# Eight v chains and all imaginary-row chains in pairs on 64 rows each, and the gate product on GpSimd and ScalarE

## The chip, the cores and the metric

The kernel runs on one core of one Trainium2 chip. The core has TensorE for matmuls (PE in the profile, with its weight loads as PEld), VectorE (DVE), ScalarE (ACT), GpSimd (POOL) and SyncE (SP), which issues most DMAs. The metric is the device time of the core in microseconds (us), the median of several executions; less is better.

## The reference, and what is computed

Two branches over the same x (2048 tokens, 512 wide) are mixed by a gate. Cut to what matters:

```
g = sigmoid((x * gate_w).sum(-1, keepdims=True))
a = x @ dft_hid_re.T ;  b = x @ dft_hid_im.T            # per token
y = dft_seq_re @ a - dft_seq_im @ b                     # over the 2048 tokens
q, k, v = split(x @ wqkv)                               # 32 heads of 16
o = softmax(q k^T / 4) v ;  m = o @ wo
out = g * y + (1 - g) * m
```

The places that the change touches are `v`, the rows `b` ("imaginary rows") and the sum inside the gate. The softmax here needs row maxima of the scores, which the kernel computes by separate score matmuls and reductions ("maxima").

## The kernel before, in words

The order of all instructions is written out by hand (`tc.manual_schedule()`): each engine works through its instructions in the order in which the Python code emits them, and the framework adds the waits between engines. All of an engine's later work stands behind an instruction that waits.

Products of float32 precision are made from three matmuls of a reduced type: each operand is split into a high part and a low part (`hi_lo`, L73 to L76: ScalarE casts the high part, VectorE or GpSimd subtracts it for the low part), and `mm3` (L78 to L81) multiplies high with high, high with low and low with high. A *chain* is the 12 matmuls of one tile of 128 tokens by 512 columns: 4 slices of the inner dimension times 3, summed in one PSUM bank.

The stages, in order: the q and k rows (until about 95 us); then, in lines 235 to 304, the part that is changed; then a long main part (from L573 on) in which the Fourier matmuls run on one half of TensorE's 128 rows while score matmuls run on the other half (`Chain.mm`, L339 to L345, slices 64 rows), with a wait put in by hand at the first matmul of each segment; then an end.

The part that is changed runs two loops over the 16 token tiles, s = 0 to 15:

- L259 to L268, the v chains. Each uses all 128 rows and a bank of `psS` (3 banks). ScalarE (L267) and VectorE (L268) each copy one half of the bank into `vt`.
- L280 to L301, the chains of imaginary rows. The same matmuls with other weights (`wch`, `wcl`). Then, in the order of emission: `hi_lo` of the bank into a tile `bt` (ScalarE casts, VectorE subtracts), a store of `bt` to DRAM (512 KB, SP), a load of a gate row block `xa[s + 2]` (256 KB, SP), and the gate product of block s by one VectorE instruction that multiplies and sums (L293). For s = 2 to 5 one slice of `wo` is split as well into a tile `wt` (ScalarE casts, GpSimd subtracts), stored, and only then is the next slice of `wo` loaded (L294 to L299). For s = 6 to 9 `split(1)` does one slice of the real Fourier weights, `wre` (cast on ScalarE, subtract on GpSimd); the first of these calls also issues the loads of all four. `bt` and `wt` share a pool name, `hl`, with two buffers.

From the eleventh v chain on, `visit` (L247 to L257) follows each chain ahead of its evacuation: it emits the score matmuls of two maxima tiles for both heads (four matmuls of 48 rows, those of head 0 on rows 0 to 47 and those of head 1 on rows 64 to 111) and their four reductions on VectorE (`a_tile`, L197 to L211). There are 22 visits, 44 maxima tiles (`LEAD`). Three of the four score banks are of `psA`, the fourth is the bank of `psD`. After 32 tiles the maxima of a half are complete, and two deferred steps (`m_parts`, `m_rows`) spread them into the stacks `qs`.

After the last chain, L302 runs what is deferred, and the main part begins with six matmuls at L343 on all 128 rows into the bank `psD`.

Of the kernel before, what the change touches and what calls it, by code (L numbers as in the profile page):

```python
# [9 lines left out]
F32 = mybir.dt.float32  # L10
F32R = mybir.dt.float32r
AF = mybir.ActivationFunctionType
ALU = mybir.AluOpType
AX = mybir.AxisListType

P = 128
S = 2048
D = 512
# [3 lines left out]
KT = D // P  # L22
NT = S // P
UNITS = NP * 32
LEAD = 44
# [6 lines left out]
def mix_kernel(ctx: ExitStack, tc: tile.TileContext, xa_t, xa, wqkv, w_hid, w_seq, wo, gate_w, out):  # L32
# [5 lines left out]
    nc = tc.nc  # L38
    ctx.enter_context(tc.manual_schedule())

    psS = ctx.enter_context(tc.tile_pool(name="psS", bufs=3, space=PSUM))
    psA = ctx.enter_context(tc.tile_pool(name="psA", bufs=3, space=PSUM))
    psO = ctx.enter_context(tc.tile_pool(name="psO", bufs=1, space=PSUM))
    psD = ctx.enter_context(tc.tile_pool(name="psD", bufs=1, space=PSUM))
# [6 lines left out]
    b_d = [dram.tile([P, 2, D], F32, name=f"b{s}") for s in range(NT)]  # L51
# [4 lines left out]
    wo_d = [dram.tile([P, 2, D], F32, name=f"wo{kt}") for kt in range(KT)]  # L56
# [5 lines left out]
    z = const.tile([P, NT], F32, name="z")  # L62
# [8 lines left out]
    xab = [const.tile([P, 4, 2, D], F32R, name=f"xab{tb}", tag=f"xab{tb}") for tb in range(4)]  # L71
    acc = psO.tile([P, 512], F32, name="acc")

    def hi_lo(hi, lo, src, lo_eng=None):
        nc.scalar.copy(hi, src)  # L75
        (lo_eng or nc.vector).tensor_tensor(lo, src, hi.bitcast(F32), ALU.subtract)  # L76

    def mm3(ps, sh, sl, mh, ml, first, last):  # L78
        nc.tensor.matmul(ps, sh, mh, start=first, stop=False)  # L79
        nc.tensor.matmul(ps, sh, ml, start=False, stop=False)  # L80
        nc.tensor.matmul(ps, sl, mh, start=False, stop=last)  # L81

    right = tc.tile_pool(name="st1", bufs=1, side="right", reuse_waits="tile")
    st1 = right.__enter__()
    wv = [[const.tile([P, D], F32R, name=f"wv{v}{kt}", tag=f"w{4 * v + kt}") for kt in range(KT)] for v in range(2)]
    wch = st1.tile([P, KT, D], F32R, name="wch")
    wcl = st1.tile([P, KT, D], F32R, name="wcl")

    gwb = st1.tile([P, D], F32, name="gwb")
# [3 lines left out]
    def staged(src):  # L93
        raw = st1.tile([P, D], F32, name="raw", bufs=RAW)
        nc.sync.dma_start(raw, src)
        return raw
# [4 lines left out]
    def load_ahead():  # L101
        while todo and len(loaded) < RAW - 1:
            hi, lo, src, lo_eng, shape = todo.pop(0)
            loaded.append((hi, lo, staged(src), lo_eng, shape))

    def split(n):

        for _ in range(n):
            load_ahead()
            if loaded:  # L110
                hi, lo, raw, lo_eng, shape = loaded.pop(0)
                hi_lo(hi, lo, raw.rearrange("p (s t) -> p s t", s=4) if shape else raw, lo_eng)
            load_ahead()
# [7 lines left out]
    def bank():  # L121
        nonlocal banks
        banks += 1
        return (psS if banks % 2 else psA).tile([P, 512], F32, name="s" if banks % 2 else "a")


    with tc.tile_pool(name="qk", bufs=1, reuse_waits="tile") as pool:
        wh = pool.tile([P, 2, KT, D], F32R, name="wh")
        wl = pool.tile([P, 2, KT, D], F32R, name="wl")
# [27 lines left out]
        for tb in range(4):  # L157
            for c in range(2):
# [9 lines left out]
                for ct in range(4):  # L168
                    ps = bank()
# [25 lines left out]
    deferred = []  # L195
    a_left = {}

    def a_tile(i, h, ps=None):
        p, j = divmod(i, 64)
        qt, kb = divmod(j, 4)  # L200
        if ps is None:
            ps = psA.tile([P, 512], F32, name="a")
        r = slice(64 * h, 64 * h + 48)
        nc.tensor.matmul(ps, qs[p % 2][r, qt * P:(qt + 1) * P], ks[p % 2][r, kb * 512:(kb + 1) * 512],  # L204
                         start=True, stop=True)
        user = nc.vector.tensor_reduce(mx[p % 2][:, h, qt, kb:kb + 1], ps, AX.X, ALU.max)  # L206
        hf = j // 32
        a_left[p, hf] = a_left.get((p, hf), 64) - 1
        if not a_left[p, hf]:
            deferred.extend((partial(m_parts, p, hf), partial(m_rows, p, hf)))  # L210
        return user  # L211
# [18 lines left out]
    def run_deferred():  # L230
        while deferred:
            deferred.pop(0)()


    ones = st1.tile([2, 2 * D], F32, name="hl", bufs=2)
    nc.gpsimd.memset(ones, 1.0)
    nc.gpsimd.memset(vt[:, :, :, 16:17], 1.0)
    for i in range(2):
# [3 lines left out]
    xgs = {s: staged(xa[s]) for s in range(2)}  # L242
    wos = [staged(wo[:, 0])]
    load_stacks(0)
    a_next = 0

    def visit(i):  # L247

        nonlocal a_next
        if i < 10 or a_next == LEAD:  # L250
            return
        if deferred:
            deferred.pop(0)()
        for j in range(2):
            for h in range(2):
                a_tile(a_next, h, psD.tile([P, 512], F32, name="d") if j and h else None)
            a_next += 1  # L257

    for s in range(NT):  # L259
        t = xab[s // 4][:, s % 4]  # L260
        ps = psS.tile([P, 512], F32, name="s")
        for kt in range(KT):
            r = slice(kt * P, (kt + 1) * P)
            mm3(ps, t[:, 0, r], t[:, 1, r], wv[0][kt], wv[1][kt], kt == 0, kt == KT - 1)
        visit(s)
        pv = ps.rearrange("p (r h d) -> p r h d", h=2, d=DH)
        nc.scalar.copy(vt[:, s, :, 0:16], pv[:, :, 0])  # L267
        nc.vector.tensor_copy(vt[:, s, :, 17:33], pv[:, :, 1])  # L268

    def spare(i, dt, name):  # L270

        return const.tile([P, 4, P], dt, name=name, tag=f"w{i}")
# [4 lines left out]
        add(wre[0][kt], wre[1][kt], w_hid[0, :, kt], nc.gpsimd)  # L277

    ab = [xab[s // 4][:, s % 4] for s in range(NT)]
    for s in range(NT):  # L280
        t = ab[s]
        ps = psS.tile([P, 512], F32, name="s")
        for kt in range(KT):
            r = slice(kt * P, (kt + 1) * P)
            mm3(ps, t[:, 0, r], t[:, 1, r], wch[:, kt], wcl[:, kt], kt == 0, kt == KT - 1)
        visit(NT + s)
        bt = st1.tile([P, 2, D], F32R, name="hl", bufs=2)
        hi_lo(bt[:, 0], bt[:, 1], ps)
        nc.sync.dma_start(b_d[s], bt.bitcast(F32))
        if s + 2 < NT:  # L290
            xgs[s + 2] = staged(xa[s + 2])
        xg = xgs.pop(s)
        nc.vector.scalar_tensor_tensor(xg, xg, 1.0, gwb, op0=ALU.mult, op1=ALU.mult, accum_out=z[:, s:s + 1])  # L293
        if 2 <= s < 2 + KT:  # L294
            wt = st1.tile([P, 2, D], F32R, name="hl", bufs=2)
            hi_lo(wt[:, 0], wt[:, 1], wos.pop(0), nc.gpsimd)
            nc.sync.dma_start(wo_d[s - 2], wt.bitcast(F32))
            if s + 1 < 2 + KT:
                wos.append(staged(wo[:, s - 1]))  # L299
        elif s >= 2 + KT:  # L300
            split(1)  # L301
    run_deferred()  # L302
    assert a_next == LEAD
    right.__exit__(None, None, None)
# [108 lines left out]
    oh, yp, wos = {}, {}, []  # L413
# [438 lines left out]
```

## Time and profile before

| | before |
|---|---|
| median of 3 runs | 1758.53 us (1757.90 to 1759.54) |
| the profiled execution, its time | 1756.66 us |
| the profiled execution, its span | 1754.8 us |
| mean granted clock of TensorE | 0.994 |
| PE busy | 1728.3 us (98%) |
| DVE busy | 1366.6 us (78%) |
| ACT busy | 1154.1 us (66%) |
| POOL busy | 447.2 us (25%) |

The profile is of one execution. Busy time counts an instruction from its start to its end; matmuls overlap, so a busy PE is not one at its peak. A timeline row reads: start, duration, engine, line, operation, output <- input, shape, count, and in brackets the idle time of the engine ahead of it and what ended that. A window row gives the busy time of PE, PEld, DVE, ACT and POOL with counts, then the granted clock, the share of the DMA engines and their GB/s. An SPq row is the issue of a DMA, not its landing.

### The profile page before, as it was taken

Reading aid. Unit: us, or ns where it says so; the run is one execution under the profiler, and the core shown is the slowest. Engines: PE = TensorE matmul, PEld = TensorE weight load, DVE = VectorE, ACT = ScalarE, POOL = GpSimd, SP = SyncE. Lnnn points to the kernel's source line nnn. Section 1 sums busy time; section 2 is a strip of 40 time slices with the busy share of each in tenths; the row PEclk is TensorE's granted clock in tenths of the full one; section 3 lists DMA queues with packets and bytes.
Section 4 is the critical chain, followed back from the end, with each engine's and each line's share of the span. In section 5 each row is a group of like instructions: output and inputs, shape, how many; then the busy total and the mean of one; then the engine's idle time right before and its main releaser. Section 6 shows DMA issues by size and latency. Waiting matters only on the chain.

```text
span 1754.8 us, 32881 instructions
## 1 busy us (share of the span) xinstructions
PE 1728.3 (98%) x12721; PEld 1041.1 (59%) x12721; DVE 1366.6 (78%) x2299; ACT 1154.1 (66%) x2258; POOL 447.2 (25%) x561
## 2 busy tenths in 40 slices
PE   8999899999999999999999999999999999999997
PEld 7886554446666666566666665666666656544443
DVE  5228878888888888888888888888888888899933
ACT  5211267776767777777677677776776777677785
POOL 0110222232223233322222243332333343200111
PEclk9999899999999999999999999999999999999998
DMA  9754620314132153414146434224142534560113
GB/s 290 236 111 144 225 35 7 56 26 73 44 69 66 47 114 92 74 54 79 44 74 235 94 116 106 69 62 76 49 80 68 123 97 92 184 148 8 42 41 109
DMA packets 82348, 164.79 MB, mean 94 GB/s; under 512 B 19712, under 2 KB 19968, under 8 KB 78352
## 3 DMA queue, kind: packets, MB, share of 16 engines
q1 hardware_dynamic: 77840, 162.30, 36.5%
q8 instruction: 100, 1.64, 0.4%
q0 software_dynamic: 4352, 0.39, 0.3%
q14 instruction: 56, 0.46, 0.1%
HBM read 107.47 MB, written 54.52 MB: 92 GB/s over the span
## 4 chain that ended last, share of the span: by engine, by line
PE 94%; DVE 2%; ACT 2%; DMA 1%; issue 0%; SPq 0%; POOL 0%; DVEq 0%; ACTq 0%; POOLq 0%
PE d L343 35%; PE acc L635 26%; PE s L626 12%; PE a L204 11%; PE s L79 2%; PE s L80 2%; PE s L81 2%; ACT pt L627 1%; DVE mx L206 1%; PE a L79 1%; PE a L80 1%; PE a L81 1%; DMA b<-hl 1%; PE a L343 1%; ACT y L359 0%
## 5 line engine op out<-in xcount | busy, mean ns | idle before, releaser
L206 DVE TENSOR_REDUCE mx<-a 128x1 f32<-128x512 f32 x2026 | 1244.2, 681 | 243.6 <-PE a L204 229.9
L627 ACT ACTIVATE pt<-s 128x512 f32<-128x512 f32 x2008 | 1026.2, 620 | 392.2 <-PE s L626 323.3
L204 PE MATMUL a<-ks,qs 48*128 48x512 f32 x2026 | 814.1, 419 | 3.7 <-DVE mx L206 3.3
L626 PE MATMUL s<-qs,ks 50*128 50x512 f32 x2008 | 769.9, 413 | 0.8 <-DMA qs<-mt 0.5
L343 PE MATMUL d<-xab,ch 64*128 64x512 f32 x2016 | 648.4, 396 | 0.0
L635 PE MATMUL acc<-pt,vt 128*17 128x512 f32 x4096 | 501.7, 597 | 0.0
L343 PEld LDWEIGHTS d<-xab,ch 64*128 64x128 f32 x2016 | 365.9, 184 | 126.6 <-DVE mx L206 60.4
L626 PEld LDWEIGHTS s<-qs,ks 50*128 50x128 f32 x2008 | 366.6, 184 | 109.6 <-ACT pt L627 29.9
L204 PEld LDWEIGHTS a<-ks,qs 48*128 48x128 f32 x2026 | 366.9, 185 | 78.6 <-DVE mx L206 48.7
L343 PE MATMUL d<-xab,cl 64*128 64x512 f32 x1008 | 399.3, 396 | 0.0
L343 PEld LDWEIGHTS d<-xab,cl 64*128 64x128 f32 x1008 | 185.5, 184 | 65.3 <-DVE mx L206 40.8
L327 POOL CAST ch<-craw 128x512 fp32r<-128x512 f32 x126 | 77.4, 614 | 555.1 <-PE d L343 179.8
L635 PEld LDWEIGHTS acc<-pt,vt 128*17 128x17 f32 x4096 | 90.3, 96 | 205.8 <-issue 205.8
L328 POOL TENSOR_TENSOR cl<-craw,ch 128x512 fp32r<-128x512 f32 x126 | 162.4, 1289 | 10.2
L227 POOL DMA_DIRECT2D qs<-mt x128 | 72.0, 568 | 160.8 <-DVE mt L223 152.3
L343 PE MATMUL d<-wre,xab 64*128 64x512 f32 (+1 forms) x348 | 94.9, 405 | 5.0 <-ACT pt L627 2.5
L343 PEld LDWEIGHTS d<-wre,xab 64*128 64x128 f32 (+1 forms) x348 | 59.9, 185 | 42.5 <-issue 26.1
L343 PE MATMUL d<-wo_hl,o_hl 64*128 64x512 f32 (+1 forms) x261 | 70.9, 397 | 0.0
L343 PEld LDWEIGHTS d<-wo_hl,o_hl 64*128 64x128 f32 (+1 forms) x261 | 47.1, 185 | 15.9 <-issue 12.0
L75 ACT CAST hl<-s 128x512 fp32r<-128x512 f32 x32 | 18.8, 586 | 56.2 <-PE s L81 48.7
L76 DVE TENSOR_TENSOR hl<-s,hl 128x512 fp32r<-128x512 f32 x32 | 22.0, 686 | 32.1 <-ACT hl L75 32.1
L218 POOL CAST nhl<-nm 128x16 fp32r<-128x16 f32 x32 | 6.3, 197 | 150.9 <-DVE nm L215 150.9
(124 smaller groups left out, 930.1 us busy)
## 6 DMA issues: line engine op xcount, KB each, us to landing
craw<-w_seq SPq DMA_DIRECT2D x128, 256.0 KB
qk<-hl SPq DMA_DIRECT2D x32, 512.0 KB
qs<-qk SPq DMA_DIRECT2D x96, 128.0 KB
ks<-qk SPq DMA_DIRECT2D x96, 128.0 KB
b<-hl SPq DMA_DIRECT2D x16, 512.0 KB
xab<-b SPq DMA_DIRECT2D x16, 512.0 KB
o<-oe SPq DMA_DIRECT2D x62, 128.0 KB
oh<-nh SPq DMA_DIRECT2D x12, 512.0 KB
```

Of the source, the lines that this page charges most:

```text
L79: nc.tensor.matmul(ps, sh, mh, start=first, stop=False)
L80: nc.tensor.matmul(ps, sh, ml, start=False, stop=False)
L81: nc.tensor.matmul(ps, sl, mh, start=False, stop=last)
L204: nc.tensor.matmul(ps, qs[p % 2][r, qt * P:(qt + 1) * P], ks[p % 2][r, kb * 512:(kb + 1) * 512], start=True, stop=True)
L206: user = nc.vector.tensor_reduce(mx[p % 2][:, h, qt, kb:kb + 1], ps, AX.X, ALU.max)
L227: (nc.sync, nc.gpsimd)[h].dma_start(rows.rearrange("v (q b c) -> v b q c", q=8, b=4)[:, b], mt[hf][32 * b + h:32 * b + 32:2])
L327: nc.gpsimd.tensor_copy(h1, raw)
L328: nc.gpsimd.tensor_tensor(l1, raw, h1.bitcast(F32), ALU.subtract)
L343: i = nc.tensor.matmul(self.ps, st[r], mv[r], start=not self.begun, stop=stop)
L626: nc.tensor.matmul(ps, ks[p % 2][rr, kt * P:(kt + 1) * P], qs[p % 2][rr, q0:q0 + 512], start=True, stop=True)
L627: return nc.scalar.activation(pts[u][:, 2 * qb + h], ps, AF.Exp, bias=0.0, scale=DH ** -0.5)
L635: nc.tensor.matmul(acc[32 * j:32 * j + 17], vt[:, kt, p, 16 * h:16 * h + 17], pt[:, j], start=kt == 0, stop=kt == NT - 1)
```

## The change

Three things are changed between lines 235 and 302.

1. The v chains of s = 8 to 15 and all 16 imaginary-row chains run in groups of four, A, B, C, D, each with a bank of its own (three of `psS`, and `psD` for s % 4 = 3). Each matmul of 128 rows becomes two of 64 rows. A group has four *phases*: A with B, first half; C with D, first half; A with B, second half; C with D, second half. In a phase 12 steps each issue one matmul of the one chain on one half of the rows and one of the other chain on the other half; in the second half the two chains have changed sides. The first matmul of a second-half phase is given a wait by hand: for the last maxima reduction of the phase before it (two matmuls on different rows but in one bank would otherwise be open at a time).
2. `visit` is gone. Each phase from the second on, 22 of them, has two maxima tiles of both heads inside: after its fourth step and after its tenth. The fourth score bank of a phase is now `acc`.
3. The evacuation of two chains follows the second-half phase, one after the other (`b_done(s)`, then `b_done(s + 1)`). In it the gate product is made by GpSimd (the product) and ScalarE (a copy with a sum) in place of the VectorE instruction. The pool name `hl` has four buffers in place of two.

```diff
-    ones = st1.tile([2, 2 * D], F32, name="hl", bufs=2)
+    ones = st1.tile([2, 2 * D], F32, name="hl", bufs=4)
...
-    def visit(i):
...
+    def x_mm(s, wh, wl):
         t = xab[s // 4][:, s % 4]
-        ps = psS.tile([P, 512], F32, name="s")
         for kt in range(KT):
-            r = slice(kt * P, (kt + 1) * P)
-            mm3(ps, t[:, 0, r], t[:, 1, r], wv[0][kt], wv[1][kt], kt == 0, kt == KT - 1)
-        visit(s)
+            h1, l1 = (t[:, v, kt * P:(kt + 1) * P] for v in range(2))
+            yield from ((h1, wh[kt]), (h1, wl[kt]), (l1, wh[kt]))
...
+    def b_done(s, ps):
+        bt = st1.tile([P, 2, D], F32R, name="hl", bufs=4)
         hi_lo(bt[:, 0], bt[:, 1], ps)
         nc.sync.dma_start(b_d[s], bt.bitcast(F32))
         if s + 2 < NT:
             xgs[s + 2] = staged(xa[s + 2])
         xg = xgs.pop(s)
-        nc.vector.scalar_tensor_tensor(xg, xg, 1.0, gwb, op0=ALU.mult, op1=ALU.mult, accum_out=z[:, s:s + 1])
+        nc.gpsimd.tensor_tensor(xg, xg, gwb, ALU.mult)
+        nc.scalar.activation(xg, xg, AF.Copy, accum_out=z[:, s:s + 1])
         if 2 <= s < 2 + KT:
-            wt = st1.tile([P, 2, D], F32R, name="hl", bufs=2)
+            wt = st1.tile([P, 2, D], F32R, name="hl", bufs=4)
             hi_lo(wt[:, 0], wt[:, 1], wos.pop(0), nc.gpsimd)
             nc.sync.dma_start(wo_d[s - 2], wt.bitcast(F32))
             if s + 1 < 2 + KT:
                 wos.append(staged(wo[:, s - 1]))
         elif s >= 2 + KT:
             split(1)
+
+    made, user = 0, None
+
+    def phase(pair, half, maxima):
+        nonlocal a_next, user
+        before, user = user, None
+        for j in range(12):
+            for x, (ps, ops, done) in enumerate(pair):
+                st, mv = ops[j]
+                r = slice(64 * (half ^ x), 64 * (half ^ x) + 64)
+                i = nc.tensor.matmul(ps, st[r], mv[r], start=not half and not j, stop=half == 1 and j == 11)
+                if not j and not x and half:
+                    tc.add_manual_dep(i.ins, before.ins.name,
+                                      mybir.DependencyInfo(mybir.DependencyClass.Sync, mybir.DependencyReason.DATA))
+            if maxima and j in (3, 9):
+                for h in range(2):
+                    user = a_tile(a_next, h, acc if h and j == 9 else None)
+                a_next += 1
+        if half:
+            for ps, ops, done in pair:
+                done(ps)
+        if deferred:
+            deferred.pop(0)()
+
+    def pairs_of(tiles, wh, wl, done):
+        nonlocal made
+        tiles = list(tiles)
+        for i in range(0, len(tiles), 4):
+            new = []
+            for s in tiles[i:i + 4]:
+                ps = psS.tile([P, 512], F32, name="s") if s % 4 < 3 else psD.tile([P, 512], F32, name="d")
+                new.append((ps, list(x_mm(s, wh, wl)), partial(done, s)))
+            for half in range(2):
+                for pair in (new[:2], new[2:]):
+                    phase(pair, half, 0 < made and a_next < LEAD)
+                    made += 1
+
+    for s in range(8):
...
+    pairs_of(range(8, NT), *wv, v_done)
...
+    pairs_of(range(NT), *([w[:, kt] for kt in range(KT)] for w in (wch, wcl)), b_done)
     run_deferred()
```

More of the change, by code (lines that the diff above doesn't have):

```diff
@@ L245, in mix_kernel, with v_done @@
     a_next = 0
-    def visit(i):
[L249 to L259, printed above, removed]
+    def x_mm(s, wh, wl):
         t = xab[s // 4][:, s % 4]
-        ps = psS.tile([P, 512], F32, name="s")
         for kt in range(KT):
-            r = slice(kt * P, (kt + 1) * P)
-            mm3(ps, t[:, 0, r], t[:, 1, r], wv[0][kt], wv[1][kt], kt == 0, kt == KT - 1)
-        visit(s)
+            h1, l1 = (t[:, v, kt * P:(kt + 1) * P] for v in range(2))
+            yield from ((h1, wh[kt]), (h1, wl[kt]), (l1, wh[kt]))
+    def v_done(s, ps):
         pv = ps.rearrange("p (r h d) -> p r h d", h=2, d=DH)
@@ L268, in mix_kernel @@
         nc.vector.tensor_copy(vt[:, s, :, 17:33], pv[:, :, 1])
+    def b_done(s, ps):
+        bt = st1.tile([P, 2, D], F32R, name="hl", bufs=4)
+        hi_lo(bt[:, 0], bt[:, 1], ps)
+        nc.sync.dma_start(b_d[s], bt.bitcast(F32))
+        if s + 2 < NT:
+            xgs[s + 2] = staged(xa[s + 2])
+        xg = xgs.pop(s)
+        nc.gpsimd.tensor_tensor(xg, xg, gwb, ALU.mult)
+        nc.scalar.activation(xg, xg, AF.Copy, accum_out=z[:, s:s + 1])
+        if 2 <= s < 2 + KT:
+            wt = st1.tile([P, 2, D], F32R, name="hl", bufs=4)
+            hi_lo(wt[:, 0], wt[:, 1], wos.pop(0), nc.gpsimd)
+            nc.sync.dma_start(wo_d[s - 2], wt.bitcast(F32))
+            if s + 1 < 2 + KT:
+                wos.append(staged(wo[:, s - 1]))
+        elif s >= 2 + KT:
+            split(1)
@@ L270, in spare @@
+    for s in range(8):
+        ps = psS.tile([P, 512], F32, name="s")
+        ops = list(x_mm(s, *wv))
+        for i, (st, mv) in enumerate(ops):
+            nc.tensor.matmul(ps, st, mv, start=not i, stop=i == len(ops) - 1)
+        v_done(s, ps)
+    pairs_of(range(8, NT), *wv, v_done)
     def spare(i, dt, name):
@@ L279, in mix_kernel @@
     ab = [xab[s // 4][:, s % 4] for s in range(NT)]
[L280 to L294, printed above, removed]
-            wt = st1.tile([P, 2, D], F32R, name="hl", bufs=2)
[L296 to L301, printed above, removed]
+    pairs_of(range(NT), *([w[:, kt] for kt in range(KT)] for w in (wch, wcl)), b_done)
     run_deferred()
```

## The prediction

> **What bounds the kernel now.** First the chain that ended last, on the page, then the windows over the changed stretch (the columns are the stretch, its length, busy time of PE, PEld, DVE, ACT, POOL, then clock, DMA share and GB/s).
>
> ```profile
> PE 94%; DVE 2%; ACT 2%; DMA 1%; issue 0%; SPq 0%; POOL 0%; DVEq 0%; ACTq 0%; POOLq 0%
> ```
> ```profile
> 124.80:143.60 18.80, 18.80 (x85) 12.66 (x84) 14.18 (x26) 2.30 (x6) 0.00 (x0) 1.00 0.00 1
> 143.60:164.90 21.30, 21.30 (x96) 14.55 (x94) 19.84 (x37) 3.59 (x6) 2.59 (x2) 1.00 0.52 178
> 164.90:194.80 29.90, 26.57 (x81) 16.67 (x80) 19.80 (x39) 6.83 (x12) 8.47 (x9) 0.83 0.73 251
> 194.80:213.85 19.05, 19.05 (x85) 12.66 (x84) 18.48 (x37) 3.53 (x6) 2.33 (x4) 1.00 0.58 194
> 213.85:216.30 2.45, 0.02 (x2) 0.05 (x1) 2.45 (x5) 0.00 (x0) 0.00 (x0) 1.00 0.55 217
> ```
>
> TensorE sets the end (94% of the chain), so what the changed stretch gains or loses reaches the end whole: behind it PE is full. Inside the stretch there are three regimes. In the v chains (first row) PE is full and VectorE has room. In most of the imaginary rows (second and fourth) VectorE is nearly full too. In the middle (third row) PE idles 3.3 us and the clock falls to 0.83. Last, PE waits 2.4 us at the border to the main part.
>
> ```profile
> 121.85 0.39 PE L81 MATMUL s<-wv,xab 128*128 128x512 f32 x1
> ...
> 124.57 0.39 PE L81 MATMUL s<-wv,xab 128*128 128x512 f32 x1
> 124.89 0.73 PE L204 MATMUL a<-ks,qs 48*128 48x512 f32 x3
> ...
> 128.50 0.73 PE L204 MATMUL a<-ks,qs 48*128 48x512 f32 x3
> ```
> ```profile
> 150.26 0.73 PE L204 MATMUL a<-ks,qs 48*128 48x512 f32 x3
> ...
> 153.92 0.73 PE L204 MATMUL a<-ks,qs 48*128 48x512 f32 x3
> ```
>
> A v chain without a visit takes 2.72 us (last matmul to last matmul, 12 at 0.2265); with one 3.61, an imaginary row 3.66. Five chains from 164.90 to 194.80 took 29.9 where 18.3 was due: 11.6 us lost.
>
> **The new phase on PE.** The rate of matmuls side by side on 64 rows is shown by the main part:
>
> ```profile
> 401.68 0.39 PE L343 MATMUL d<-xab,chl 64*128 64x512 f32 x1
> 401.69 0.40 PE L626 MATMUL s<-qs,ks 50*128 50x512 f32 x1
> ...
> 404.47 0.38 PE L343 MATMUL d<-xab,ch 64*128 64x512 f32 x1
> 404.62 0.43 PE L204 MATMUL a<-ks,qs 48*128 48x512 f32 x1
> ```
>
> Both sides go through 12 intervals between the first and the last pair of rows: 2.79 and 2.93 us, so 0.238 per slot of two. That is one full-row matmul plus 5%; the pairing gives the arithmetic itself nothing. What it removes is the change between full and half rows: a visit costs 3.61 - 2.72 = 0.89, of which two slots of maxima are 0.48, so 0.41 goes to the change, 22 times, 9 us. A phase with maxima is 14 slots, 3.33 us, one without 12, 2.86. Eight phases of v (the first without maxima) and 16 of rows (the last without) are 332 slots: 79.0 us. Bounds: 0.2265 gives 75.2, 0.244 gives 81.0; I take the middle, which averages both sides. Only one change of rows is left, about 0.1.
>
> **The wait put in by hand.** The first matmul of a second half waits for the last maxima reduction of the phase before.
>
> ```profile
> 125.42 1.89 DVE L206 TENSOR_REDUCE mx<-a 128x1 f32<-128x512 f32 x3 [2.30 <-PE a L204]
> 127.22 0.68 DVE L206 TENSOR_REDUCE mx<-d 128x1 f32<-128x512 f32 x1
> ```
>
> With VectorE idle (2.30) a reduction begins 0.53 after its score matmul (124.89 to 125.42); they follow each other at 0.60 and the last takes 0.68. So the last of two ends 1.81 after the scores begin. In the new phase the scores after the tenth step are followed by two steps only: 3 slots, 0.71 us. PE then stands 1.1 us, and with the restart (weights not yet loaded; between 0 and 0.2, I take 0.15) 1.25. Behind this instruction, PE being in order, stands everything that PE has. Two waits per group, 6 groups: 12 waits, 15 us if VectorE is never late, less where another stall covers one. Bounds 1.0 and 1.4 each.
>
> So v gives 110 slots, 26.2, plus 4 waits, 5.0: from 116.6 (124.8, the end of the eleventh chain, less three chains) to 148.0, where before the rows began at 143.6. Nothing pays for this 4.4 us: the six visits removed were worth 2.5.
>
> **The gate product.** VectorE is relieved:
>
> ```profile
> 149.54 0.68 DVE L76 TENSOR_TENSOR hl<-s,hl 128x512 fp32r<-128x512 f32 x1
> 150.14 0.68 DVE L293 SCALAR_TENSOR_TENSOR raw<-raw,gwb 128x512 f32<-128x512 f32 x1
> 150.75 0.08 DVE L293 DVE_READ_ACCUMULATOR raw<-raw,gwb 128x1 f32 x1
> 150.79 1.89 DVE L206 TENSOR_REDUCE mx<-a 128x1 f32<-128x512 f32 x3
> ```
>
> It gives up 0.65 a row (150.14 to 150.79), 10.4 us in all. Four reductions, a subtraction and this were 3.65 of the 3.66 period; without it 3.0 a row is left against 3.33 of PE a phase. The path in the rows is therefore PE, its waits, and the evacuations. The new GpSimd product and ScalarE copy with a sum are not in the trace; nearest are GpSimd's subtraction and ScalarE's casts:
>
> ```profile
> 170.81 1.28 POOL L76 TENSOR_TENSOR hl<-raw,hl 128x512 fp32r<-128x512 f32 x1 [5.46 <-ACT hl L75]
> ```
> ```profile
> 170.11 0.62 ACT L75 CAST hl<-raw 128x512 fp32r<-128x512 f32 x1 [4.13 <-DMA raw<-wo]
> 171.37 0.59 ACT L75 CAST hl<-s 128x512 fp32r<-128x512 f32 x1 [0.64 <-DMA b<-hl]
> 176.32 0.62 ACT L75 CAST hl<-raw 128x512 fp32r<-128x512 f32 x1 [4.36 <-DMA raw<-wo]
> 177.57 0.59 ACT L75 CAST hl<-s 128x512 fp32r<-128x512 f32 x1 [0.63 <-DMA b<-hl]
> 184.17 0.62 ACT L75 CAST wre<-raw 128x512 fp32r<-128x512 f32 x1 [6.01 <-DMA raw<-w_hid]
> ```
>
> I take 1.3 and 0.62 (0.6 to 0.7). Their busy time is harmless; their place is not. The sum of row s stands on ScalarE ahead of the cast of row s + 1, and both rows of a pair are evacuated at once, so the bank of D comes free only after the product of C, which waits for its load.
>
> ```profile
> 172.12 0.32 SPq L297 DMA_DIRECT2D wo<-hl  x1
> 172.49 0.42 SPq L95 DMA_DIRECT2D raw<-wo  x1
> ```
>
> A 256 KB load is used 3.83 us after its issue (172.49 to the cast at 176.32). Count from the end of a group's second half of A and B: last reduction 1.15, subtraction to 1.9, store issue, load of the gate block of C issued 2.3, landed 6.2, product 7.5, sum 8.1, the cast of a split 8.75, cast of D 9.4, its subtraction 10.1. PE wants D at 1.25 + 3.33 + 3.33 = 7.9. So D is about 2.2 late between the first and second group of rows, and about 2.6 (a cast of the ninth row's split stands ahead instead) between third and fourth. Bounds for the landing: 1.7 by the 2 KB rows below, 4.54 by the store below; 3.83 is the same load from the same queue.
>
> ```profile
> qs<-mt POOLq DMA_DIRECT2D x128, 2.0 KB, 1.7
> ```
> ```profile
> 166.73 4.54 DMA b<-hl
> ```
>
> **The loads of wo and wre.** Before, two loops went round at some 6.2 us in the middle: store of `bt` (4.54), cast, subtraction, because `hl` had two buffers; and load of `wo` (3.83), cast 0.7, GpSimd 1.3, store issue 0.37 (172.12 to 172.49). Four buffers open the first. The second stays: each load is still issued behind the store of the slice before. Placed on the new schedule: the first group ends at 163.8, the first slice is cast at 167.5, the others at 173.7, 179.9, 186.1. The cast of row 6 stands behind the last, 186.7, though its phase ended at 182.2; its subtraction is done at 188.0; then store, gate load, and the first `wre` load is issued at 189.2, cast at 193.4; the cast of row 7 is behind that one (194.0), its subtraction ends 195.3. PE finishes A and B of the third group at 185.5 and wants D: 9.8 us idle. The phase after it runs at a low clock:
>
> ```profile
> 191.74 0.63 PE L80 MATMUL s<-wcl,xab 128*128 128x512 f32 x1
> 192.16 0.63 PE L81 MATMUL s<-wch,xab 128*128 128x512 f32 x1
> ```
>
> 0.42 against 0.23, so 14 slots cost 2.7 more. VectorE is held by the same subtractions, and its reductions then run late, which I put at 0.15 on two waits and take back 0.55 on the one behind the slow phase.
>
> [...]
>
> **The end.** Before, the first matmul of the main part waited for a reduction:
>
> ```profile
> 216.28 1.63 PE d L343 x6
> ```
>
> Now it wants the bank of row 15: the gate load of row 14 is issued 2.2 after the previous pair, a phase and a wait (4.1) ahead of the end; landed, multiplied, summed, cast and subtracted (3.83 + 1.3 + 0.7 + 0.7 + 0.7) it is free 5.3 after the last matmul. The maxima steps to `qs` are issued as often as before; behind products on GpSimd, but needed only after this point, so free.
>
> **Sum**, from 116.64 to the first matmul at L343: slots 79.0, waits 14.75, D late 2.3 + 9.8 + 2.6 = 14.7, low clock 2.7, end 5.3, change of rows 0.1: 116.55. Before it was 216.28 - 116.64 = 99.64. That is +16.9 on the profiled 1754.8 span and 1756.66 time, 1773.6. The median of runs lies 1.9 above this profile: 1758.5 + 17 = 1775.5.
>
> **Rivals.** *Faster: the two-buffer loop was what lost the time.* If the store of `bt`, which the chain of waits does show (4.54), held ScalarE and the loads land in about 2 us, D is never late and the 11.6 goes. Then slots 79.0, waits 15.0, end 3, change 0.1: 97.1, or -2.5; with 0.2265 and 1.0 it is 90.3, or -9.3. Centre -6, 1752.5. Against it: the casts name the load of `wo` as what came last (4.13 and 4.36), and that load isn't touched. It decides if loads land below some 2.5 us.
>
> *Partly late.* Landing at 3 us and no hold by `wre`: D late 2 + 5 + 1, end 4, no slow phase: 79 + 15 + 8 + 4 = 106, +6.4, 1765.
>
> *The waits lower the clock.* If 1.25 idle in every 4.6 us brings the low clock, as 190 to 194 had it, over a third of the slots, 110 times 0.19 is 21 more: 1796. Against: from 143.6 to 164.9 gaps of 0.4 a visit left it at 1.00. [...]
>
> *Not side by side.* If the halves took turns, 332 more slots, +79 and more: over 1850. The rows at 401 to 404 speak against it for this very shape.
>
> **Chances.** Forecast 0.66 (own range 1768 to 1784: landing and waits at their ends), faster rival 0.16, partly late 0.11, low clock 0.05, no pairing 0.02. About 0.2% (3.5 us) is what a measurement can tell from no change. Of the faster rival 0.12 is beyond it and 0.04 within, of partly late 0.02 within: faster 0.12, same 0.06, slower 0.82. Leaving out most of the faster rival and the two dearest, the range is 1757 to 1787.
>
> **What would show it.** Right: PE idle a good 1 us ahead of each second half, released by a reduction of line 206; one idle stretch of some 10 us around the third group of rows, followed by matmuls of 0.63; the first full-row L343 matmul near 233; ScalarE waiting for GpSimd and for raw loads ahead of casts of banks. Wrong: second halves that begin without a gap, casts of D that wait only for PE, or that first matmul ahead of 216.

## The result, and the profile after

| | before | after |
|---|---|---|
| median of the runs | 1759.03 us (4 runs, 1757.90 to 1761.78) | 1776.77 us (4 runs, 1774.11 to 1777.84) |
| ratio, 95% interval | | 1.0100 (1.0087 to 1.0112) |
| profiled execution, time and span | 1756.66 and 1754.8 us | 1777.84 and 1775.3 us |

The change makes the kernel 17.7 us, 1%, slower; 1775.5 was forecast. Where the time goes is read first from the chain of waits on the page after, then from windows over the changed stretch (columns as before).

```profile
PE 93%; ACT 2%; DVE 2%; DMA 2%; POOL 1%; issue 1%; SPq 0%; DVEq 0%; ACTq 0%; POOLq 0%
```

Before, PE had 94% and DMA 1%, GpSimd and issue none: the chain now passes through waits for loads and for GpSimd. The windows say where:

```profile
116.60:147.00 30.40, 26.73 (x222) 20.96 (x224) 19.57 (x34) 2.39 (x8) 0.00 (x0) 1.00 0.00 1
147.00:164.00 17.00, 15.16 (x128) 11.65 (x126) 13.50 (x23) 3.51 (x9) 0.69 (x1) 1.00 0.22 78
164.00:183.20 19.20, 16.09 (x127) 11.56 (x124) 11.73 (x19) 6.10 (x14) 8.19 (x7) 1.00 0.77 256
183.20:195.20 12.00, 1.09 (x8) 0.31 (x4) 1.47 (x3) 2.93 (x6) 3.76 (x4) 0.65 0.75 271
195.20:203.00 7.80, 7.22 (x39) 5.40 (x41) 5.13 (x10) 1.23 (x3) 3.85 (x6) 0.67 0.31 103
203.00:227.80 24.80, 19.57 (x156) 14.06 (x152) 16.29 (x26) 8.18 (x21) 11.50 (x11) 1.00 0.46 151
227.80:232.60 4.80, 0.06 (x1) 0.06 (x1) 1.38 (x2) 1.78 (x5) 2.52 (x2) 0.84 0.81 323
```

PE has gaps in every stage of the stretch, and one where it hardly works at all: 12 us from 183.2 to 195.2 with 1.1 us of matmuls, followed by 7.8 us with a mean clock of 0.67. The timeline of PE names what ended the gaps (the brackets):

```profile
128.11 0.50 PE L288 MATMUL s<-wv,xab 64*128 64x512 f32 x1 [0.92 <-DVE mx L206]
128.12 0.50 PE L288 MATMUL d<-wv,xab 64*128 64x512 f32 x1
128.45 0.39 PE L288 MATMUL s<-wv,xab 64*128 64x512 f32 x1
...
131.47 1.07 PE L288 MATMUL s<-wv,xab 64*128 64x512 f32 x8
...
167.13 0.49 PE L288 MATMUL d<-wch,xab 64*128 64x512 f32 x1 [1.22 <-DVE hl L76]
...
186.41 0.53 PE L288 MATMUL s<-wch,xab 64*128 64x512 f32 x1 [2.69 <-DVE hl L76]
195.17 0.79 PE L288 MATMUL d<-wch,xab 64*128 64x512 f32 x1 [8.23 <-DVE hl L76]
...
215.44 0.49 PE L288 MATMUL d<-wch,xab 64*128 64x512 f32 x1 [2.34 <-DVE hl L76]
...
232.54 2.93 PE L375 MATMUL d<-wre,xab 128*128 128x512 f32 x6 [4.82 <-DVE hl L76]
```

The first row is one of twelve: a second half waits for a maxima reduction. The second begins 0.01 later, so the two halves do run side by side. The rows from 167.13 on wait for the subtraction that empties a bank (`s` is bank C, `d` bank D). The last row is the first matmul of the main part, which began at 216.28 before: 16.3 us later, and its six matmuls, at a low clock (0.50), take 2.93 where they took 1.63. From here on I call its start the *border*; it dates a whole stretch in one row. The profiled executions do not reach the changed stretch at the same time: the ninth v chain begins between 116.42 and 117.89, so border times of two runs compare only to some 1.5 us. *Counted* means from that beginning to the border: 99.6 before (116.64 to 216.28) and 116.0 after (116.53 to 232.54). That nothing later pays it back is seen in the transposition of the maxima (L223), first before, then after, early and late in the main part:

```profile
262.79 0.20 DVE L223 STREAM_TRANSPOSE mt<-nhl 128x32 f32<-128x32 f32 x1
...
1680.93 0.21 DVE L223 STREAM_TRANSPOSE mt<-nhl 128x32 f32<-128x32 f32 x1 [0.60 <-POOL nhl L219]
```
```profile
281.42 0.20 DVE L223 STREAM_TRANSPOSE mt<-nhl 128x32 f32<-128x32 f32 x1
...
1699.50 0.21 DVE L223 STREAM_TRANSPOSE mt<-nhl 128x32 f32<-128x32 f32 x1 [0.60 <-POOL nhl L219]
```

It is 18.6 us late at both. (The profiled spans differ by 20.5; some 2 us of that arise behind 1700 us in this execution, which is the longest of its four, and are not explained here.)

Who holds the banks is seen on ScalarE after, around the long gap:

```profile
184.54 0.62 ACT L75 CAST hl<-raw 128x512 fp32r<-128x512 f32 x1 [2.44 <-DMA raw<-wo]
185.06 0.58 ACT L75 CAST hl<-s 128x512 fp32r<-128x512 f32 x1
187.80 0.63 ACT L267 ACTIVATE raw<-raw 128x512 f32<-128x512 f32 x1 [2.16 <-POOL raw L266]
188.34 0.19 ACT L267 ACTIVATION_READ_ACCUMULATOR raw<-raw 128x1 f32 x1
193.23 0.62 ACT L75 CAST wre<-raw 128x512 fp32r<-128x512 f32 x1 [4.71 <-DMA raw<-w_hid]
193.76 0.58 ACT L75 CAST hl<-d 128x512 fp32r<-128x512 f32 x1
```

Bank C (185.06) is cast right behind the last slice of `wo`, which waited for its load; bank D (193.76) right behind the sum of the row before it, which waited for GpSimd, and the first slice of `wre`, which waited 4.7 us for its load. PE had been through with D since 180.

### The profile page after: what moved, and what is told of

Its sections match the earlier page's. It is cut to its first block, busy times and chain, and to the rows that moved or that the text cites. A ratio compares the mean times of both kernels' runs of the same rounds, so it can differ in the third digit from the quotient of the medians.

```text
span 1775.3 us, 33476 instructions
## 1 busy us (share of the span) xinstructions
PE 1724.4 (97%) x13009; PEld 1044.6 (59%) x13009; DVE 1358.9 (77%) x2267; ACT 1163.3 (66%) x2290; POOL 466.4 (26%) x577
## 4 chain that ended last, share of the span: by engine, by line
PE 93%; ACT 2%; DVE 2%; DMA 2%; POOL 1%; issue 1%; SPq 0%; DVEq 0%; ACTq 0%; POOLq 0%
PE d L375 35%; PE acc L667 26%; PE s L658 11%; PE a L204 11%; PE s L288 1%; ACT pt L659 1%; PE s L319 1%; DVE mx L206 1%; PE s L79 1%; PE s L80 1%; PE a L79 1%; PE a L80 1%; PE s L81 1%; PE a L81 1%; PE d L288 1%; DMA raw<-wo 1%
## 5 line engine op out<-in xcount | busy, mean ns | idle before, releaser
L288 PE MATMUL s<-wch,xab 64*128 64x512 f32 x192 | 44.8, 406 | 9.8 <-DVE mx L206 7.1
L75 ACT CAST hl<-s 128x512 fp32r<-128x512 f32 x28 | 16.3, 584 | 52.9 <-PE s L288 30.8
```

Source lines behind the costliest of these rows:

```text
L288: i = nc.tensor.matmul(ps, st[r], mv[r], start=not half and not j, stop=half == 1 and j == 11)
```

## The experiments

Theory: three costs, each new or moved: the wait by hand behind a late reduction; the place of sums and splits on ScalarE ahead of a bank's cast; the loads that those splits wait for. Rivals: that the two buffers, not the loads, had lost the 11.6 us before; that VectorE is the limit, so that a removed wait only moves; that the pairs themselves make the gap.

**e1: maxima earlier in the phase.**

```diff
-            if maxima and j in (3, 9):
+            if maxima and j in (0, 4):
...
-                    user = a_tile(a_next, h, acc if h and j == 9 else None)
+                    user = a_tile(a_next, h, acc if h and j == 4 else None)
```

> The two maxima tiles of a phase stand behind its first and fifth step in place of its fourth and tenth; nothing else. My theory: the last reduction is then over before the phase ends, so the idle time of some 0.92 us (plus restart) ahead of each second half goes. In the v chains all four waits are bare: 4 x 1.05 = 4.2 us gained; in the first group of rows two more, 2.1; behind that the late banks take back most of it, and two waits late in the stretch may give 1 each. 6 to 9 us less than the changed kernel: about 1769. Rival (VectorE is the limit, the wait only moves to the score banks): within 2 us of the changed kernel.

Ratio to before 1.0072 (1.0044 to 1.0100), median 1771.93: 4.8 us less than the changed kernel, between the 6 to 9 expected and the rival's 2, from four runs that lie 8 us apart. The profiled one is the slowest of them (1777.14); its border is at 231.60, 0.9 us earlier and 2.1 counted. The twelve waits are gone from PE's timeline and the first slice of `wo` is cast at 160.69 in place of 165.26. But the loads take most of the gain back (D of the third group waits 8.92 and comes at 192.00, 3.2 earlier), and much of the rest goes to the clock: windows behind two gaps of e1.

```profile
191.90:198.50 6.60, 6.50 (x28) 4.70 (x30) 5.23 (x11) 1.23 (x3) 4.01 (x7) 0.50 0.36 122
212.70:219.20 6.50, 6.47 (x26) 4.63 (x28) 4.84 (x8) 0.00 (x0) 2.53 (x2) 0.52 0.37 121
```

Half clock for 6.5 us twice; of these two places the changed kernel had it only at the first (0.50 from 195.0 to 200.4; 1.00 from 215 to 222). This does not settle what the waits cost: that needs a stretch without the long gap (e8 and e9).

**e2: both banks first.** `b_done` is cut behind the store; products, sums and splits of both rows follow as `b_rest`.

```diff
             for ps, ops, done in pair:
                 done(ps)
+            if pair[0][2].func is b_done:
+                for ps, ops, done in pair:
+                    b_rest(*done.args)
```

> Both banks of a pair are cast, subtracted and stored first; gate product, sum and the splits of both rows follow. Loads and waits are untouched. My theory: the order on ScalarE is what makes bank D late. The stalls of 1.2 us ahead of the second group of rows and 2.3 ahead of the fourth go, the 2.7 + 8.2 ahead of the third become one of about 4 (both casts still stand behind the last split of wo), the slow clock there mostly goes, and the 4.8 at the end becomes 2. Together 10 to 14 us less than the changed kernel: about 1765. Rival (it is the late loads themselves, wherever the casts stand): 3 us or less.

Ratio 1.0065 (1.0039 to 1.0091), median 1770.97, 5.8 us less than the changed kernel where 10 to 14 were expected; border 227.44. D is never late on its own any more, and the gap in the third group is 5.96, but about half of the gain is lost again at a place that wasn't foreseen (VectorE, then PE):

```profile
193.19 0.68 DVE L206 TENSOR_REDUCE mx<-acc 128x1 f32<-128x512 f32 x1
201.96 0.21 DVE L223 STREAM_TRANSPOSE mt<-nhl 128x32 f32<-128x32 f32 x1 [8.09 <-POOL nhl L219]
```
```profile
204.59 0.79 PE L290 MATMUL s<-wch,xab 64*128 64x512 f32 x1 [7.14 <-DVE mx L206]
```

The deferred steps of the maxima stand on GpSimd behind products and splits that wait for loads, and VectorE's reductions stand behind the transposition.

**e3: the gate back on VectorE.**

```diff
-        nc.gpsimd.tensor_tensor(xg, xg, gwb, ALU.mult)
-        nc.scalar.activation(xg, xg, AF.Copy, accum_out=z[:, s:s + 1])
+        nc.vector.scalar_tensor_tensor(xg, xg, 1.0, gwb, op0=ALU.mult, op1=ALU.mult, accum_out=z[:, s:s + 1])
```

> The gate product goes back to one VectorE instruction; all else as changed. My theory: ScalarE loses the sums, so the cast of D is earlier by up to 2 us where no split stands ahead, but VectorE now waits for the gate block and has 0.65 us a row more: within 3 us of the changed kernel, about 1775. Rival (VectorE had been the limit of the rows, and relieving it is the useful part of the change): 5 us or more slower than the changed kernel, 1782 and up.

Ratio 1.0065 (1.0042 to 1.0088), median 1770.80; border 228.48. Both sides of the expectation missed: the kernel is 6 us faster by medians than the changed one (4.3 counted), where a time within 3 us of it, or one 5 us slower, was expected. So this part of the change costs some 4 us where it was put, not for its work but for its place: the waits for D fall from 1.22 to 0.24, from 2.34 to 0.40, and the end from 4.82 to 3.02:

```profile
212.54 0.50 PE L287 MATMUL d<-wch,xab 64*128 64x512 f32 x1 [0.40 <-DVE hl L76]
...
228.48 2.93 PE L374 MATMUL d<-wre,xab 128*128 128x512 f32 x6 [3.02 <-DVE hl L76]
```

**b4: the kernel before with four buffers.**

```diff
-    ones = st1.tile([2, 2 * D], F32, name="hl", bufs=2)
+    ones = st1.tile([2, 2 * D], F32, name="hl", bufs=4)
```

(and so for `bt` and `wt`.)

> The kernel before, with four buffers of hl in place of two and nothing else. My theory: the loss of 11.6 us in the middle of its rows comes from the loop over the loads of wo, whose period of some 6.2 us the buffers do not touch: 0 to 3 us less than before, about 1757. Rival (the loop of store, cast and subtraction over two buffers lost it): about 11 us less, 1747.

Ratio 1.0002 (0.9990 to 1.0014), border 217.05: nothing gained. ScalarE now never waits for a store, and waits as long for the loads:

```profile
154.65 0.62 ACT L75 CAST hl<-raw 128x512 fp32r<-128x512 f32 x1
...
164.16 0.62 ACT L75 CAST hl<-raw 128x512 fp32r<-128x512 f32 x1 [5.75 <-DMA raw<-wo]
...
185.70 0.62 ACT L75 CAST wre<-raw 128x512 fp32r<-128x512 f32 x1 [7.62 <-DMA raw<-w_hid]
```

The rival that the buffers had lost the time falls, although the chain of waits before ran through `DMA b<-hl`. That two loops of nearly equal length stood side by side, as the prediction had it, fits this.

**e5, b5: the loads out of the way**, in the changed kernel and in the kernel before (b5 has the four buffers of b4 too).

```diff
-        raw = st1.tile([P, D], F32, name="raw", bufs=RAW)
+        raw = st1.tile([P, D], F32, name="raw", bufs=RAW + 2)
...
-    wos = [staged(wo[:, 0])]
+    wos = [staged(wo[:, kt]) for kt in range(KT)]
...
+        if 4 <= s < 8:
+            wo_split(s - 4)
...
-        if 2 <= s < 2 + KT:
-            wt = st1.tile([P, 2, D], F32R, name="hl", bufs=4)
...
-        elif s >= 2 + KT:
+        if s == 1:
+            load_ahead()
+        elif 4 <= s < 8:
             split(1)
```

> The changed kernel with its weight loads out of the way: all four slices of wo are loaded together ahead of the v chains and split behind the fifth to eighth v chain, the loads of wre are issued at row 1 and split at rows 4 to 7 (two more buffers for raw loads). Waits and the order at the banks stay. Theory (the loads hold ScalarE, and so bank D, in the middle of the rows): the idle stretches of 2.7 and 8.2 us and the slow clock behind them go; about 1.2 a group of late D, the twelve waits and a late end of some 4.8 stay. First matmul of the main part near 217 to 220 in place of 232.5, time about 1762. Rival (the stretch is made by the pairs and their order, not by loads): 5 us or less gained.

> The kernel before with the same moved loads and splits (and four buffers of hl); full rows, visits and the gate product on VectorE as they were. Theory: its loss of 11.6 us in the rows comes from the loads as well and goes: about 1747, first matmul of the main part near 205. Rival (the loss is VectorE's, which is full in the rows): 4 us or less gained.

e5: ratio 1.0039 (1.0025 to 1.0053), median 1765.07; border 221.65, 10.9 us earlier than after (11.4 counted), and 3 us above the 1762 expected. The long gap shrinks to 2.81, the end stays:

```profile
186.44 0.49 PE L291 MATMUL d<-wch,xab 64*128 64x512 f32 x1 [2.81 <-DVE hl L76]
...
221.65 2.56 PE L378 MATMUL d<-wre,xab 128*128 128x512 f32 x6 [4.87 <-DVE hl L76]
```

b5: ratio 0.9936 (0.9917 to 0.9956), median 1747.81; border 204.61, 11.7 earlier than before (also counted), where 11.6 had been lost. So both kernels lose about the same to these loads, and the loads explain the gap, not the slowdown.

**e6, e7: banks first as well, then early maxima as well** (the edits of e5 and e2; then those and e1).

> As e5_loads_early, and both banks of a pair are emptied ahead of gate product, sum and splits as in e2_banks_first. Theory: bank D is never late; 332 slots at 0.231, twelve waits of 1.1 and an end of 2 make 92: first matmul of the main part near 209, time about 1752. Rival (GpSimd, which now has products, splits and the steps of the maxima, holds VectorE as in e2_banks_first): 1757 or more, with VectorE waiting for GpSimd at the transposition of the maxima.

> As e6_loads_banks, and the maxima stand behind steps one and five as in e1_maxima_early. Theory: the waits were worth their 0.92 us idle once nothing else covers them: 332 slots, an end of 2 and some 0.6 a group where VectorE is just late, 81: first matmul of the main part near 198, 9 to 11 us less than e6_loads_banks, time about 1741, and so faster than both kernels. Rival (VectorE takes over as the limit): 4 us or less gained on e6_loads_banks.

e6: ratio 0.9975 (0.9965 to 0.9985), median 1755.64, border 213.68: between the theory (1752, 209) and the rival (1757), with a trace of e2's hold (1.79 ahead of one second half). e7: ratio 0.9955 (0.9937 to 0.9973), median 1751.41, border 206.59: 4 us gained of the 9 to 11 expected, and slower than b5, which has no pairs. At the border 7.1 are gained, but 3.3 are left at the first matmuls of L675 behind it (222.63 against 225.90): the last sums of the gate hold the first exponentials, PE waits 1.51 for them, and the six full-row matmuls from 214.05 take 2.93 where those from 208.84 took 1.66. What it lost ahead of the border stands on PE and VectorE:

```profile
176.99 0.50 PE L293 MATMUL s<-wch,xab 64*128 64x512 f32 x1 [3.08 <-DVE hl L76]
...
212.44 0.61 PE L666 MATMUL s<-qs,ks 50*128 50x512 f32 x1 [1.51 <-ACT pt L667]
```
```profile
185.28 0.21 DVE L223 STREAM_TRANSPOSE mt<-nhl 128x32 f32<-128x32 f32 x1 [2.64 <-POOL nhl L219]
```

The waits of 3.08 and 2.64 go back to GpSimd, which has the products and the splits in one queue.

**e8, e9, b6: the gate in the v chains.** To the edits of e7 (for e9: without that of e1), and to b5 for b6:

```diff
-        raw = st1.tile([P, D], F32, name="raw", bufs=RAW + 2)
+        raw = st1.tile([P, D], F32, name="raw", bufs=RAW + 4)
...
+    def gate_row(r):
+        xg = xgs.pop(r)
+        nc.gpsimd.tensor_tensor(xg, xg, gwb, ALU.mult)
+        nc.scalar.activation(xg, xg, AF.Copy, accum_out=z[:, r:r + 1])
+        if r + 4 < NT:
+            xgs[r + 4] = staged(xa[r + 4])
...
-        xg = xgs.pop(s)
-        nc.gpsimd.tensor_tensor(xg, xg, gwb, ALU.mult)
-        nc.scalar.activation(xg, xg, AF.Copy, accum_out=z[:, s:s + 1])
```

(`gate_row` is called for two rows behind each of the last eight v chains; in b6 the lines taken out are the VectorE instruction.)

> As e7_all_three, and the gate product and sum of all 16 rows move from the rows into the paired v chains, still on GpSimd and ScalarE (two rows behind each of the last eight v chains, after both banks are emptied; four more raw buffers than the changed kernel). Theory: what e7_all_three still lost (3.1 us for a pair of banks, a slow clock, VectorE 2.6 us behind GpSimd, exponentials waiting for the sums) was the gate's place among the splits; without it PE runs through: 332 slots of 0.231, an end of 2, some 2 for VectorE just late: first matmul of the main part near 198, time about 1741, 6 us under b5_before_loads_early. Rival (VectorE or the small waits take it over again): 1747 or more.

> As e8_gate_in_v with the maxima back behind the fourth and tenth step. Theory: the twelve waits now stand bare, 0.92 idle and 0.1 to 0.2 of restart each: 10 to 13 us more than e8_gate_in_v, about 1753. Rival (the wait by hand is covered by other work): 3 us or less more.

> As b5_before_loads_early, with the gate in the v chains on GpSimd and ScalarE as in e8_gate_in_v. Full rows and visits stay. Theory: VectorE is no longer full in the rows, but PE with the change between full and half rows is: a row 3.61 in place of 3.66, so 1 us gained, 1747. Rival (the gate was the limit of the rows): 5 us or more gained.

| | pairs | maxima behind steps | median, us | ratio to before (95%) | border | counted |
|---|---|---|---|---|---|---|
| e8 | yes | 1 and 5 | 1741.33 | 0.9891 (0.9874 to 0.9908) | 200.55 | 82.7 |
| e9 | yes | 4 and 10 | 1751.68 | 0.9952 (0.9939 to 0.9966) | 210.16 | 93.7 |
| b6 | no | visits | 1747.41 | 0.9925 (0.9912 to 0.9938) | 205.08 | 88.0 |

All three times came out as the theory had them; the 1 us that b6 was to gain on b5 is too small to be told (0.4 by medians, none when counted), but its rival of 5 us falls. Where the ninth v chain begins, of e8 and e9:

```profile
117.89 3.03 PE L301 MATMUL s<-wv,xab 64*128 64x512 f32 x24
```
```profile
116.42 3.26 PE L301 MATMUL s<-wv,xab 64*128 64x512 f32 x25
```

PE's rows at the border, of e8, e9 and b6:

```profile
200.55 1.65 PE L390 MATMUL d<-wre,xab 128*128 128x512 f32 x6 [1.98 <-DVE hl L76]
```
```profile
205.10 0.50 PE L301 MATMUL s<-wch,xab 64*128 64x512 f32 x1 [0.92 <-DVE mx L206]
210.16 2.81 PE L390 MATMUL d<-wre,xab 128*128 128x512 f32 x6 [1.99 <-DVE hl L76]
```
```profile
205.08 2.61 PE L357 MATMUL d<-wre,xab 128*128 128x512 f32 x6 [2.43 <-DVE mx L206]
```

This is the clean trial of the pairs. With nothing else in the way, and the maxima where the change puts them, pairs take 5.7 us longer to the border than full rows with visits (93.7 against 88.0); with the maxima early they take 5.3 less. e8 is the fastest kernel of the study: 20 us below the runs of before that were timed with it (median 1761.45), and 35 below after.

## Why the prediction was right, point by point

**Slots.** Right in kind, 2% too dear. In a second half of v the 13 slots from 128.45 to 131.47 take 0.232 each; in the first group of rows 13 slots from 150.05 to 153.09 take 0.234. The 0.238 came from the busier main part. 332 slots: some 77.5 in place of 79.0.

**The wait by hand.** Right. PE stands idle twelve times, 0.90 to 0.99 us in eleven of them and 0.58 in the one behind the slow phase, where the prediction took some back. Since a matmul's row outlasts its slot here (0.39 against 0.232), the whole cost is the cycle between two waits (123.69 to 128.11) less its 14 slots, 4.42 - 3.25 = 1.17, against 1.25. The v chains end at about 146.8 where 148.0 was forecast and 143.6 was before: 3.2 lost of the 4.4 forecast. e8 against e9 shows the price with no other stall about: 11.1 us counted for twelve (9.6 by the border alone, as e8 began 1.5 later). Twelve times 1.17 would be 14.0; e8 loses some 1.5 of it at three places where VectorE is itself just late (0.26 to 0.53 idle), and the rest was not traced.

**Late banks.** Right in mechanism and total: 2.3 (2.2 in its working), 9.8 and 2.6 were forecast in the second, third and fourth group, 14.7 in all; 1.22, 2.69 + 8.23 and 2.34 idle were measured, 14.5. Part of the match is luck: the first is half of its forecast, the middle 1.1 above. The last cast of `wo` was put at 186.1 and came at 184.54; the first of `wre` was put at 193.4 and came at 193.23, because the way between them took 8.7 in place of 7.3. e2, e3 and e5 each take their share of the late banks away (5.7, 4.3 and 11.4 us counted).

**Low clock.** The phase behind the gap was put 2.7 us up; the window from 195.2 shows the clock at 0.67, and the 12 slots from 195.17 to 200.43 cost 2.4 more than at full clock. The low clock behind the 4.8 us gap at the border (2.93 against 1.63 in the first six matmuls) is not in the sum of the prediction. It takes the 16.3 at the border to 18.6 later, 2.3 us, and covers what the slots had been priced too high: that the total came within about 1 us is partly luck.

**The end.** 5.3 forecast, 4.82 measured. The border was forecast at 233.2 (116.64 + 116.55) and came at 232.54. Slots 77.5, waits 13.8, late banks 14.5, low clock 2.4 and the end 4.8 make 113.0 of the 116.0 counted; the other 3, in part the restarts behind late banks, are not split up.

**The deferred steps called free.** Wrong as a statement, though it cost nothing here: in after, the transposition at 201.51 did not wait. The likely reason is that the late banks held VectorE longer: in e2 they do so less, and VectorE then waits 8.09 us for the steps, 7.14 of it seen on PE.

**The rivals.** The two buffers: refuted by b4. Partly late and not side by side: refuted by the rows above (8.23 idle and a clock of 0.50 behind it, from 195.0 to 200.4; two halves 0.01 apart). That the short waits lower the clock: the windows to 183.2 all show 1.00 with a wait in every other phase.

## What to carry to other kernels

When work is moved to an engine that is idle on average, ask what stands behind it in that engine's order: here a sum and a split that wait for loads stood ahead of the cast that frees a bank, and with two banks freed at once the second also waits for what the first brings with it. A wait put in for safety should name an event that is long past; moving its source five steps ahead was worth 10 us (e8 against e9), the whole difference between a loss and a gain for the pairs. And a stall that both versions share (the loads, 11 to 12 us in each) hides what a change is worth; take it out of both before judging.

## What the runs showed of the hardware

The low clock, in windows of 0.4 us of the two main profiles: before, the granted clock reads 0.50 from 187.6 to 194.0, with 0.77 and 0.70 in the windows at the two edges; after, it reads 0.50 from 186.8 to 200.0 (0.92 and 0.51 at the edges) and from 231.2 to 237.6 (0.89 and 0.58). The windows next to these read 1.00. Estimated from the means at the edges, that is 6.8 us before, 13.7 and 6.8 after. In the first stretch of after the clock had fallen behind the gap of 2.69, with PE's one row at 186.41, and so ahead of the gap of 8.23.

When it read 1.00 again, PE had worked for some 5.2 us (after, from 195.17), 5.4 (after, from 232.54), 6.9 (before, from 187.35) and 7.3 (e1, from 192.00, by its windows of 3 us: 0.50, 0.50 and 0.79 from 192 to 201, then 1.00). In e3 the six matmuls from 228.48 take 2.93, the next six, from 232.15, 1.66.

The slow rows before stand behind a gap of 1.93 (187.35). Gaps of 1.99 us (e9's border, 2.81 for its six matmuls) and 2.68 (e1, at 212.72, a clock of 0.52 to 219.2) were followed by the low clock or its slow rows as well, and gaps of 1.98 (e8's border, 1.65 for the six), 2.34 (after, at 215.44, 1.00 to 222) and 2.43 (before's border, 1.00 from 216 to 223) were not. So in these runs the length of a gap alone does not tell.

The sum on ScalarE is two instructions, 0.63 for the copy and 0.19 for reading the sum (after, 187.80 and 188.34), as the one on VectorE was (0.68 and 0.08, before, 150.14 and 150.75).
